# Seven-product stage of a Fourier and sliding-window kernel: second halves lag ten products, low parts earlier, half of the gate moved beside it

## The chip, the cores and the metric

The kernel runs on one core of a Trainium2 chip. The metric is the device time of one execution in microseconds. Before the change its median is 891.25 us over three runs (891.09 to 891.96). One execution was also profiled; its own time was 883.99 us, and the profile spans 882.3 us of it. Five engines run side by side: PE multiplies matrices, DVE (VectorE), ACT (ScalarE) and POOL (GpSimd) work on elements, SP only issues transfers. POOL and ACT issue transfers too. The profile shows PE's weight loads apart, as PEld.

## The reference

With x of 2048 rows by 512 columns, the output mixes two branches row by row:

```
g = sigmoid((x * gate_w).sum(-1))
a = x @ dft_hid_re.T ;  b = x @ dft_hid_im.T            # 2048 x 512 each
A = dft_seq_re @ a - dft_seq_im @ b                     # 2048 x 2048 by 2048 x 512, twice
q, k, v = x @ wqkv      (32 heads of 16, scale 1/4)
B = softmax(q k^T, keys j with 0 <= i - j < 256) v @ wo
out = g * A + (1 - g) * B
```

All inputs and the output are float32.

## The kernel before, in words

**Numbers in two parts.** An operand of a large product is split into a high part (type fp32r, one copy or cast on ACT, called `hi` or the first half of a `big` tile) and a low part (the original minus the high part, one subtraction on DVE or POOL). A product is the sum of three: high by high, high by low, low by high.

**The dense stream.** The generator `dense` yields after each step; `halves64` is its main part. It runs every product as two halves of 64 rows, so that one matmul of an upper half and one of a lower half stand side by side on PE. A step issues one matmul of a part's first half and one of a part's second half; the second halves come `DELAY` = 6 steps later. In order, the parts are 38 of 12 steps (q and k of all heads, v), then eight pairs of 42 steps, then the products with the sequence matrices, 24 steps each. 1896 first halves make 1902 steps.

**A pair** (function `pair`) computes a and b for two blocks of 128 rows by a two-by-two block product with seven products instead of eight, six steps each. They accumulate in four places in PSUM, `o1`, `o7`, `o5`, `o6`; the first three take two products each. When a half of a product ends and others will still accumulate in the same place, `product` either calls the place's `mid` (ACT copies the sum to `U` or `V`, or DVE adds it to `V`) or lets ACT copy one column of it to `tick` (L530). The other half's first matmul waits for that copy.

**Operands of a pair.** `x_load(p)` brings 512 KB of x to a `raw` tile through POOL's queue. `x_sums(p)` makes four sums of quarters on POOL (L748 to L751). `x_split` makes four high parts on ACT (L761) and their low parts (all recorded at L142): number 0 (512 columns) and number 3 (256 columns) on DVE, 1 and 2 (512 columns) on POOL. The parts go to six places in `XT`. At a pair's end the sums of `U`, `V` and PSUM are formed on DVE (L810, L813, L835, L845) and one on POOL (`fourth`, L816), and are stored to `ab_scr`.

**Due times.** `after(n, fn)` emits `fn` n steps after now. All five engines take their instructions in the order of emission, so what stands ahead on an engine's queue delays what stands behind. `prepare` emits everything for the pairs relative to t, the first pair's first step; `b` is the start of the pair before p.

**The attention** is interleaved with the dense stream: about every seven steps a pair of score matmuls (L356), whose row minimum DVE takes at once (L360, `junk` and `ml`), and a pair of transposed scores (L415), whose exponential ACT takes (L418) and POOL masks (L420, L424); every 56 steps or so a product with v (L438).

**The gate** g needs x once more in rows: `gate_load(j)` brings two blocks of 128 rows to a `raw` tile through POOL's queue, `gate(tb)` multiplies one by the gate's weights and sums the row on DVE (L257). All 16 blocks run while q and k are computed. `home` (3072 columns) holds the q and k parts on their way out; later `load_ab` uses it for a and b on their way in (`reload`).

Of the kernel before, what the change touches and what calls it, by code (L numbers as in the profile page):

```python
# [7 lines left out]
F32 = mybir.dt.float32  # L8
# [6 lines left out]
P = 128  # L15
S = 2048
D = 512
# [24 lines left out]
AHEAD = 216  # L42
SC = 10, 14, 9, 13, 8, 12, 0, 11, 15, 4, 1, 5, 2, 6, 3, 7
# [3 lines left out]
def fnet_window_mix(ctx: ExitStack, tc: tile.TileContext, xT, xp, x, wqk, wv, wr, wi, cr, ci, wo, gw, out):  # L47
# [197 lines left out]

    def gate_load(j):
        if j == 0:
            gwb.append(ev.tile([P, D], F32, name="ev"))
            with behind("sp"):
                ld(gwb[0], bass.AP(tensor=gw.tensor, offset=gw.offset, ap=[[0, P], [1, D]]))  # L250
        GX[j] = raw_tile()
        for c in range(2):
            ld_pool(GX[j][:, HALVES[c]], x[2 * j + c])

    def gate(tb):
        t = GX[tb // 2][:, HALVES[tb % 2]]
# [68 lines left out]
    stage = [f(home[:, 512 * k:512 * k + 512]) for k in range(6)]  # L325
# [208 lines left out]
    def halves64(groups):  # L534
# [3 lines left out]
        steps.append(len(first) + DELAY)  # L538
        ends = {}
        for d, order in ((0, first), (DELAY, second)):  # L540
            for t, (part, _) in enumerate(order):
                if part.out.load:
                    ends[part.out] = max(t + d, ends.get(part.out, 0))
# [3 lines left out]
        for t in range(len(first) + DELAY):  # L547
# [3 lines left out]
            if t < len(first):  # L551
# [6 lines left out]
            if t >= DELAY:  # L558
                part_b, i_b = second[t - DELAY]
                product(part_b, 1, i_b)  # L560
# [75 lines left out]
    def dense():  # L636
# [116 lines left out]
        XSPOTS = [(k, 2) for k in range(4)] + [(k, 3) for k in range(2)]  # L753

        def x_split(n, p, k):
            def go():
                t = tiles[p, k] = XT[XSPOTS[(4 * p + k) % 6]]
                m = 256 if k == 3 else 512
                raw = (RAWS["x", p][:, :512], RAWS["s", p][:, :512],
                       RAWS["s", p][:, 512:], RAWS["x", p][:, 768:])[k]  # L760
# [4 lines left out]
        def prepare():  # L765
# [32 lines left out]
        def pair(p):  # L798
# [21 lines left out]
            def place(t, k):  # L820
                ab[t] = XT[((2, 3), (3, 3))[k]] if p == 6 else XT[XSPOTS[(26 + k) % 6]]
# [11 lines left out]
            def p7_end(o):  # L833
# [4 lines left out]
                else:  # L838
                    d = place(t2, 1)
                    after(3, nc.scalar.copy, d[:, 0], e)  # L840
# [479 lines left out]
```

## Time and profile before

| what | value |
|---|---|
| median of three runs | 891.25 us |
| profiled execution, its span | 883.99 us, 882.3 us |
| busy of the span: PE, DVE, ACT, POOL | 833.7, 578.4, 437.5, 445.7 us |
| q, k, v in `halves64` | 33.5 to 184.7 us |
| the eight pairs | 184.7 to 344.2 us |
| products with the sequence matrices in `halves64` | 344.2 to 730 us |

The bounds of the stages were found by counting the matmuls of L525, two to a step: 912 in the first stage, 672 in the pairs. Times in the views are microseconds from the start of the span, unless they say ns. In a view of waits a row is the engine and line that waited, the releaser, and the sum, the count and the longest in us.

### The profile page before, as it was taken

How to read it: one execution, taken by the hardware profiler on the slowest of the kernel's cores; microseconds unless marked ns; L12 is line 12 of the kernel's file. 1: busy time of each engine (PE TensorE's matmuls, PEld its weight loads, DVE VectorE, ACT ScalarE, POOL GpSimd, SP SyncE). 2: the span in 40 equal slices, each digit the busy share in tenths (PEclk: the TensorE clock that was granted, in tenths of full speed). 3: DMA queues.
4: the chain of work that ended last, by engine and by line, in shares of the span. 5: the costliest groups of instructions: out<-in, count | busy, mean ns of one | idle time of the engine just before them, and what ended most of it. 6: DMA issues, size and time to landing. Idle time of an engine off the chain costs nothing.

```text
span 882.3 us, 19861 instructions
## 1 busy us (share of the span) xinstructions
PE 833.7 (94%) x7202; PEld 644.6 (73%) x7202; DVE 578.4 (66%) x1558; ACT 437.5 (50%) x878; POOL 445.7 (51%) x764
## 2 busy tenths in 40 slices
PE   9999989997988887999999999999999999899998
PEld 7898756765656556677777777767777777788886
DVE  6378777866865668765676665678787626455452
ACT  6236555565444456565565555556555564231310
POOL 5005546567764785354344444446554545675530
PEclk9999999999997998999999999999999999999999
DMA  9888997884454357456564665787887566875631
GB/s 340 256 241 242 324 316 233 280 299 134 149 158 117 114 177 249 144 146 187 152 182 128 189 182 171 220 238 218 237 245 224 162 191 198 241 246 162 205 111 48
DMA packets 112434, 177.72 MB, mean 201 GB/s; under 512 B 34640, under 2 KB 44368, under 8 KB 112336
## 3 DMA queue, kind: packets, MB, share of 16 engines
q1 hardware_dynamic: 97344, 129.14, 47.4%
q0 software_dynamic: 13024, 46.14, 17.2%
q10 hardware_dynamic: 1968, 1.18, 0.5%
q8 instruction: 56, 0.92, 0.5%
q14 instruction: 42, 0.34, 0.1%
HBM read 114.56 MB, written 61.60 MB: 200 GB/s over the span
## 4 chain that ended last, share of the span: by engine, by line
PE 67%; DVE 11%; DMA 8%; issue 6%; ACT 4%; POOL 2%; SPq 1%; ACTq 0%; DVEq 0%; POOLq 0%
PE d L525 35%; PE o L438 9%; PE dc L581 8%; PE t L1145 5%; PE s L356 5%; DVE junk L360 4%; PE t L415 3%; PE d L568 2%; DMA qk_scr<-home 2%; DVE big L142 2%; DMA raw<-ci 2%; DMA ring<-qk_scr 2%; ACT pt L418 2%; DVE lo L158 1%; DMA home<-ab_scr 1%
## 5 line engine op out<-in xcount | busy, mean ns | idle before, releaser
L360 DVE CUSTOM_DVE_ANT_0 junk<-s,mask 128x384 f32<-128x384 f32 (+2 forms) x512 | 271.7, 531 | 174.8 <-PE s L356 163.7
L525 PE MATMUL d<-big,hi 64*128 64x512 f32 x1920 | 337.2, 394 | 0.0
L420 POOL TENSOR_SCALAR_AFFINE_SELECT pt<-pt 128x256 f32<-128x256 f32 x256 | 117.9, 461 | 287.5 <-ACT pt L418 221.6
L418 ACT ACTIVATE pt<-t 128x768 f32<-128x768 f32 (+2 forms) x256 | 197.6, 772 | 130.3 <-PE t L415 122.2
L525 PEld LDWEIGHTS d<-big,hi 64*128 64x128 f32 x1920 | 189.0, 187 | 27.9 <-issue 0.7
L525 PE MATMUL d<-big,lo 64*128 64x512 f32 x960 | 199.9, 394 | 0.0
L356 PE MATMUL s<-ring,ring 48*128 48x384 f32 (+2 forms) x512 | 106.8, 364 | 12.5 <-DVE ml L360 8.6
L525 PE MATMUL d<-hi,big 64*128 64x512 f32 x352 | 97.5, 408 | 10.9 <-ACT tick L530 10.8
L525 PEld LDWEIGHTS d<-big,lo 64*128 64x128 f32 x960 | 96.4, 187 | 13.4
L415 PE MATMUL t<-ring,ring 50*128 50x384 f32 (+2 forms) x512 | 95.1, 332 | 3.9 <-ACT tick L530 3.8
L424 POOL TENSOR_SCALAR_AFFINE_SELECT pt<-pt 128x256 f32<-128x256 f32 x224 | 97.3, 434 | 0.0
L157 ACT CAST hi<-raw 128x512 fp32r<-128x512 f32 x134 | 82.2, 618 | 27.6 <-DMA raw<-ci 15.4
L581 PE MATMUL dc<-big,hi 128*128 128x512 f32 x284 | 91.7, 392 | 0.0
L438 PE MATMUL o<-pt,vt 128*32 128x384 f32 (+2 forms) x1408 | 85.7, 391 | 3.0 <-DVE ml L360 2.8
L158 DVE TENSOR_TENSOR lo<-raw,hi 128x512 fp32r<-128x512 f32 x102 | 80.7, 791 | 10.1 <-ACT hi L157 9.8
L356 PEld LDWEIGHTS s<-ring,ring 48*128 48x128 f32 x512 | 58.0, 187 | 39.6 <-DVE ml L360 19.6
L525 PE MATMUL d<-big 64*128 64x512 f32 x384 | 81.2, 414 | 4.5 <-ACT tick L530 3.0
L438 PEld LDWEIGHTS o<-pt,vt 128*32 128x32 f32 x1408 | 42.5, 111 | 49.9 <-issue 30.0
L525 PEld LDWEIGHTS d<-hi,big 64*128 64x128 f32 x352 | 55.1, 191 | 23.8 <-ACT tick L530 20.3
L415 PEld LDWEIGHTS t<-ring,ring 50*128 50x128 f32 x512 | 55.3, 186 | 16.6 <-ACT tick L530 5.1
L525 PEld LDWEIGHTS d<-big 64*128 64x128 f32 x384 | 52.2, 190 | 18.0 <-ACT tick L530 15.6
L158 POOL TENSOR_TENSOR lo<-raw,hi 128x512 fp32r<-128x512 f32 x32 | 43.0, 1354 | 42.5 <-ACT hi L157 42.3
(150 smaller groups left out, 1123.4 us busy)
## 6 DMA issues: line engine op xcount, KB each, us to landing
ring<-qk_scr SPq DMA_DIRECT2D x128, 192.0 KB
qk_scr<-home SPq DMA_DIRECT2D x32, 512.0 KB
raw<-cr POOLq DMA_DIRECT2D x32, 512.0 KB, 5.2
r_scr<-ev SPq DMA_DIRECT2D x44, 256.0 KB
raw<-ci POOLq DMA_DIRECT2D x18, 512.0 KB, 6.1
qk_scr<-home SPq DMA_DIRECT2D x32, 256.0 KB
ev<-l_scr SPq DMA_DIRECT2D x32, 256.0 KB
o_scr<-ev SPq DMA_DIRECT2D x32, 256.0 KB
```

What stands on the lines that cost most here:

```text
L157: jobs.append(lambda c=c: nc.scalar.copy(hi[:, c], raw[:, c]))
L158: jobs.append(lambda c=c: (nc.gpsimd if FIN else nc.vector).tensor_sub(lo[:, c], raw[:, c], f(hi[:, c])))
L356: nc.tensor.matmul(ps[:, h, :w], ring[0][r, p, j * P:j * P + P], ring[1][r, p, k0:k0 + w], start=True, stop=True)
L360: mark("dve", nc.vector.tensor_tensor_reduce(out=junk[:, :w], in0=ps[:, h, :w], in1=mask[:, WIN - w:], scale=1.0, scalar=3e38, op0=OP.add, ...
L415: nc.tensor.matmul(ps[:, h, :w], ring[1][r, p, q0:q0 + P], ring[0][r, p, q0:q0 + w], start=True, stop=True)
L418: nc.scalar.activation(pt[:, ph, :w], ps[:, :, :w], AF.Exp, scale=-1.0)
L420: nc.gpsimd.affine_select(a, a, pattern=[[0, 2], [1, P]], compare_op=OP.is_ge, fill=0.0, base=0, channel_multiplier=-1)
L424: nc.gpsimd.affine_select(a, a, pattern=[[0, 2], [-1, P]], compare_op=OP.is_gt, fill=0.0, base=0, channel_multiplier=1)
L438: nc.tensor.matmul(o[32 * j:32 * j + 32, (a - 4 * c) * P:(e - 4 * c) * P], v[:, kb % 4, 32 * j:32 * j + 32], PT[G * NB + kb][:, j, (a - kb ...
L525: nc.tensor.matmul(o.ps, lhs[r], rhs[r], start=start, stop=end and o.left == 0, skip_group_check=True)
L581: nc.tensor.matmul(ps, w[a][:, i % 8 * 128:i % 8 * 128 + 128], ab[SC[i]][:, b], start=i == ends[0] and a + b == 0, stop=i == ends[1] and a ...
L1145: nc.tensor.matmul(ps, o[:, a, c], fin(n, b, c), start=start and c == 0 and a + b == 0, stop=c == 1 and a == 1, skip_group_check=True)
```

## The change

**Second halves.** `HOLE` = 4 empty steps are put into the list of second halves where the pairs begin, and four into the list of first halves where the products of 24 steps begin. Between the two, a second half comes ten steps after its first half. There are 1906 steps in place of 1902.

**Low parts and sums.** For the pairs from the third on, relative to `b`: load at -6 (was -8), sums at 14 (22), high parts 0, 1, 2, 3 at 12, 26, 32, 16 (26, 31, 39, 35); each low part comes three steps later as before. The first two pairs have times of their own. Parts 0 to 2 alternate between two sets of three places; part 3 has half of `XT[2, 3]` to itself.

**Gate.** The blocks 0 to 7 stay beside q and k; 8 to 15 are loaded at t + 22, 49, ... into `home` and multiplied 22 steps after their load, with a second copy of the gate's weights in `home`. `U` and `V` move from `ev` tiles to `home`, and `mid` is called at once instead of two steps later. `reload` has five places instead of six, and its casts come two steps later.

At the start of the fourth pair, PE's queue held before the change (`d` are places in PSUM, `big` and `hi`/`lo` the operands):

```order
L525 MATMUL d_3279<-hi_2730,big_561 128x512
L525 MATMUL d_3249<-big_429,big_593 128x512
L525 MATMUL d_3428<-hi_1938,big_479 128x512 [waits DVE_49]
L525 MATMUL d_3279<-hi_2730,big_561 128x512 [waits Activation_49]
L356 MATMUL s_3433<-ring1_298,ring0_297 128x384 [waits DVE_49]
```

and now:

```order
L534 MATMUL d_3402<-hi_1913,big_522 128x512 [waits DVE_49]
L534 MATMUL d_3221<-big_429,big_619 128x512
L534 MATMUL d_3402<-lo_1914,big_522 128x512
L534 MATMUL d_3221<-big_429,big_619 128x512
L365 MATMUL s_3407<-ring1_298,ring0_297 128x384 [waits DVE_49]
L365 MATMUL s_3407<-ring1_298,ring0_297 128x384
L534 MATMUL d_3402<-hi_1913,big_522 128x512
L534 MATMUL d_3221<-big_444,big_619 128x512
L534 MATMUL d_3402<-hi_1913,big_522 128x512
L534 MATMUL d_3221<-big_429,big_619 128x512
L534 MATMUL d_3402<-lo_1914,big_522 128x512
L534 MATMUL d_3252<-hi_2697,big_505 128x512 [waits Activation_49]
```

The row that waits for the copy to `tick` is the fourth of the first piece: it reopens `d_3279` one step after the last matmul of the same place's first half, which is the piece's first row. In the second piece the last matmul of the first half of `d_3252` stands two rows ahead of the first row; the row that reopens `d_3252` and waits for ACT is the last one. Four full steps and a pair of scores have come between.

On DVE, around the end of the fourth pair before the change (`junk,ml` are the row minima, 128x256 is low part 3):

```order
L813 TENSOR_TENSOR ev<-d,ev 128x512
L360 ISA junk,ml<-s,mask 128x384
L360 ISA ml 128x1
L360 ISA junk,ml<-s,mask 128x384
L360 ISA ml 128x1
L142 TENSOR_TENSOR big<-raw,big 128x256
L835 TENSOR_TENSOR ev<-d,ev 128x512
```

and around the start of a pair now:

```order
L868 TENSOR_TENSOR ev<-d,home 128x512
L266 SCALAR_TENSOR_TENSOR home,gl<-home 128x512
L143 TENSOR_TENSOR big<-raw,big 128x512
L369 ISA junk,ml<-s,mask 128x384
L369 ISA ml 128x1
L369 ISA junk,ml<-s,mask 128x384
L369 ISA ml 128x1
L143 TENSOR_TENSOR big<-raw,big 128x256
```

Low part 3 has moved from the stretch between L813 and L835, a pair's end, to the stretch behind L868, the end of the pair before; a gate (L266) stands ahead of low part 0.

POOL's queue at a pair's end, before:

```order
L72 DMA raw<-xp 128x1024
L142 TENSOR_TENSOR big<-raw,big 128x512
L816 TENSOR_TENSOR ev<-ev 128x512
L420 AFFINE_SELECT pt<-pt 128x2x128
L424 AFFINE_SELECT pt<-pt 128x2x128
L142 TENSOR_TENSOR big<-raw,big 128x512
```

and now:

```order
L143 TENSOR_TENSOR big<-raw,big 128x512
L429 AFFINE_SELECT pt<-pt 128x2x128
L433 AFFINE_SELECT pt<-pt 128x2x128
L73 DMA home<-x 128x512
L143 TENSOR_TENSOR big<-raw,big 128x512
L73 DMA raw<-xp 128x1024
L839 TENSOR_TENSOR home<-home 128x512
```

Both low parts of POOL now stand ahead of the next load of x and of `fourth`; the issue of a gate's load stands between them.

```diff
+HOLE = 4
...
+    def gate_place(tb, t):
+        GX[tb] = t
+        ld_pool(t, x[tb])
...
-    stage = [f(home[:, 512 * k:512 * k + 512]) for k in range(6)]
+    stage = [f(home[:, 512 * k:512 * k + 512]) for k in (2, 3, 0, 5, 4)]
...
-        steps.append(len(first) + DELAY)
+        at = next(i for i, p in enumerate(second) if p[0].n < 12)
+        second[at:at] = [None] * HOLE
+        at = next(i for i, p in enumerate(first) if p[0].n > 12)
+        first[at:at] = [None] * HOLE
+        steps.append(len(second) + DELAY)
...
-        XSPOTS = [(k, 2) for k in range(4)] + [(k, 3) for k in range(2)]
+        def spot(k):
+            return XT[((0, 2), (1, 2), (2, 2), (3, 2), (0, 3), (1, 3))[k % 6]]
+
+        def home_spot(k):
+            return home[:, 512 * k:512 * k + 512]
 
         def x_split(n, p, k):
             def go():
-                t = tiles[p, k] = XT[XSPOTS[(4 * p + k) % 6]]
+                t = tiles[p, k] = spot(3 * p + k) if k < 3 else XT[2, 3][:, :, p % 2 * 256:p % 2 * 256 + 256]
...
                 b = t + 42 * p - 42
-                after(t - 38 if p == 0 else t + 14 if p == 1 else b - 8, x_load, p)
-                after(b + (20 if p == 0 else 29 if p == 1 else 22), x_sums, p)
-                for k, n in enumerate((30, 35, 40, 38) if p == 1 else (26, 31, 39, 35)):
+                load, add, *splits = {0: (4, 20, 24, 30, 36, 52), 1: (14, 27, 27, 36, 40, 30)}.get(
+                    p, (-6, 14, 12, 26, 32, 16))
+                after(b + load, x_load, p)
+                after(b + add, x_sums, p)
+                for k, n in enumerate(splits):
                     x_split(b + n, p, k)
+            after(t + 20, lambda: gate_weights(f(home_spot(1))))
+            for i in range(8):
+                after(t + 22 + 27 * i, gate_place, 8 + i, f(home_spot(2 + i % 2)))
+                after(t + 44 + 27 * i, gate, 8 + i)
...
             def keep(into):
                 def go(o):
-                    u = ev.tile([P, 512], F32, name="ev")
+                    u = f(home_spot(5 - (into is U) if p < 7 else 1)) if into is U or p < 7 else ev.tile(
+                        [P, 512], F32, name="ev")
                     nc.scalar.copy(u, o.ps)
                     into.append(u)
-                return shortly(go)
+                return go
...
-            o5 = Out(shortly(p5_end), 2, mid=shortly(p5_mid))
+            o5 = Out(shortly(p5_end), 2, mid=p5_mid)
...
         def reload():
             w = [XT[dk, ss] for ss in range(2) for dk in range(4)]
-            x = [XT[XSPOTS[(28 + k) % 6]] for k in range(4)]
-            casts = [-5] * 6
...
+            x = [*map(spot, (3, 4, 5)), XT[2, 3]]
+            casts = [-5] * 5
...
-                at = max(n - 29, casts[-6] + 5)
+                at = max(n - 29, casts[-5] + 5, {8: 5, 12: 17, 0: 17}.get(sc, 0))
...
-            9: [lambda: gate_load(0)],
-            10: [lambda: gate_load(1)],
             11: [lambda: load_w(2, wqk[2])],
-            12: [lambda: gates(0, 1)],
...
+            12: [lambda: gate_load(0)],
+            14: [lambda: split_w(2), lambda: gates(0, 1)],
+            15: [lambda: gate_load(1)],
+            16: [lambda: load_w(3, wqk[3])],
+            17: [lambda: gates(2, 3)],
+            18: [lambda: split_w(3), lambda: gate_load(2)],
+            20: [lambda: gate_load(3), lambda: gates(4, 5), lambda: prepare()],
+            22: [lambda: gates(6, 7)],
```

More of the change, by code (lines that the diff above doesn't have):

```diff
@@ L244, in fnet_window_mix, with gate_weights @@
     GX = {}
+    def gate_weights(t):
+        gwb[:] = [t]
+        with behind("sp"):
+            ld(t, bass.AP(tensor=gw.tensor, offset=gw.offset, ap=[[0, P], [1, D]]))
     def gate_load(j):
         if j == 0:
[L248 to L251, printed above, removed]
+            gate_weights(ev.tile([P, D], F32, name="ev"))
+        t = raw_tile()
         for c in range(2):
-            ld_pool(GX[j][:, HALVES[c]], x[2 * j + c])
+            GX[2 * j + c] = t[:, HALVES[c]]
+            ld_pool(GX[2 * j + c], x[2 * j + c])
+    def gate_place(tb, t):
+        GX[tb] = t
+        ld_pool(t, x[tb])
     def gate(tb):
-        t = GX[tb // 2][:, HALVES[tb % 2]]
+        t = GX.pop(tb)
         nc.vector.scalar_tensor_tensor(t, t, 1.0, gwb[0], op0=OP.mult, op1=OP.mult,
@@ L537, in halves64 @@
                   for i in range(p.n)]
-        steps.append(len(first) + DELAY)
+        at = next(i for i, p in enumerate(second) if p[0].n < 12)
[3 more added lines that the diff above has]
+        steps.append(len(second) + DELAY)
         ends = {}
         for d, order in ((0, first), (DELAY, second)):
-            for t, (part, _) in enumerate(order):
-                if part.out.load:
-                    ends[part.out] = max(t + d, ends.get(part.out, 0))
+            for t, e in enumerate(order):
+                if e and e[0].out.load:
+                    ends[e[0].out] = max(t + d, ends.get(e[0].out, 0))
         fetches = {}
@@ L546, in halves64 @@
             fetches.setdefault(t - FETCH, []).append(o)
-        for t in range(len(first) + DELAY):
+        for t in range(steps[0]):
             taken[0] += 1
@@ L550, in halves64 @@
                 o.r = o.load()
-            if t < len(first):
+            if t < len(first) and first[t]:
                 part, i = first[t]
@@ L557, in halves64 @@
                 product(part, 0, i)
-            if t >= DELAY:
+            if t >= DELAY and second[t - DELAY]:
                 part_b, i_b = second[t - DELAY]
@@ L839, in p7_end @@
                     d = place(t2, 1)
-                    after(3, nc.scalar.copy, d[:, 0], e)
-                    after(6, nc.vector.tensor_sub, d[:, 1], e, f(d[:, 0]))
+                    after(8, nc.scalar.copy, d[:, 0], e)
+                    after(11, nc.vector.tensor_sub, d[:, 1], e, f(d[:, 0]))
             def p5_end(o):
@@ L885, in reload @@
             w = [XT[dk, ss] for ss in range(2) for dk in range(4)]
-            x = [XT[XSPOTS[(28 + k) % 6]] for k in range(4)]
-            casts = [-5] * 6
-            for n, sc, dst in ((27, 9, w[0]), (29, 13, w[1]), (31, 8, x[1]), (34, 12, w[2]), (37, 0, w[3]), (46, 4, w[4]),
-                               (50, 1, w[5]), (54, 5, x[0]), (60, 2, w[6]), (64, 6, w[7]), (68, 3, x[3]), (72, 7, x[2])):
-                at = max(n - 29, casts[-6] + 5)
+            x = [*map(spot, (3, 4, 5)), XT[2, 3]]
+            casts = [-5] * 5
+            for n, sc, dst in ((29, 9, w[0]), (31, 13, w[1]), (33, 8, x[1]), (36, 12, w[2]), (39, 0, w[3]), (48, 4, w[4]),
+                               (52, 1, w[5]), (56, 5, x[0]), (62, 2, w[6]), (66, 6, w[7]), (70, 3, x[3]), (74, 7, x[2])):
+                at = max(n - 29, casts[-5] + 5, {8: 5, 12: 17, 0: 17}.get(sc, 0))
                 casts.append(n)
@@ L915, in dense @@
             order[i].pre = lambda fns=fns: [fn() for fn in fns]
-        for p, k, fn in ((6, 1, pieces.load), (7, 0, lambda: (reload(), pieces.load())), (7, 1, pieces.split),
+        for p, k, fn in ((6, 4, pieces.load), (7, 0, lambda: (reload(), pieces.load())), (7, 1, pieces.split),
                          (7, 3, pieces.load), (7, 4, pieces.split), (7, 6, pieces.load)):
```

16 lines of the change are left out of this document (2 added, 14 removed).

## The prediction

> **What bounds the kernel now.** I read first the page's busy times: PE 94%, no other engine over 66%. Then the windows by stage, PE's half-height products (L525) alone; the columns are the stretch, its length, PE's and PEld's busy time with their instructions, granted clock, DMA share and GB/s:
>
> ```profile
> span 882.3 us, 19861 instructions
> ...
> PE 833.7 (94%) x7202; PEld 644.6 (73%) x7202; DVE 578.4 (66%) x1558; ACT 437.5 (50%) x878; POOL 445.7 (51%) x764
> ...
> 184.70:344.20 159.50, 114.52 (x674) 79.02 (x672) 0.97 0.53 166
> 400.00:550.00 150.00, 123.38 (x890) 81.37 (x886) 1.00 0.58 167
> 550.00:700.00 150.00, 119.53 (x860) 80.01 (x862) 1.00 0.76 222
> ```
>
> The eight pairs have 336 steps, 672 matmuls. They take 159.5 us, 0.475 us a step. Two later stretches with the same attention between the steps do 445 and 430 steps in 150 us, 0.337 and 0.349 us a step; 336 steps at those rates are 113 and 117 us. So the pairs carry 42 to 46 us that a step does not need. Where these go, the waits of PE's weight loads say, in the pairs, and in the last row in the stretch from 33.5 to 101 us (the row before it is the group of the copies to `tick` in the pairs):
>
> ```profile
> PEld d L525 <- ACT tick L530: 35.8, 51, 1.7
> PEld s L356 <- DVE ml L360: 7.9, 6, 2.6
> ...
> PEld s L376 <- DVE ml L360: 4.1, 2, 3.2
> ...
> L530 ACT COPY tick<-d 128x1 f32<-128x1 f32 x56 | 8.9, 158 | 12.1 <-PE d L525 11.7
> ...
> PEld d L525 <- ACT tick L530: 0.3, 1, 0.3
> ```
>
> 51 of the 56 copies to `tick` hold PE up in the pairs, 35.8 us in all, 0.70 us each. The same copy costs 0.3 us in all from 33.5 to 101 us, where six or more steps lie between a place's last first-half matmul and its first second-half one. In the pairs none lies between: a product has six steps and the second half comes six later. One such wait in the timeline (start, length, engine):
>
> ```profile
> 240.85 0.39 PE L525 MATMUL d<-hi,big 64*128 64x512 f32 x1
> 240.94 0.39 ACT L418 ACTIVATE pt<-t 128x256 f32<-128x256 f32 x1
> 241.22 0.40 ACT L403 COPY vt<-vr 128x256 f32<-128x256 f32 x1
> ...
> 241.51 0.17 ACT L530 COPY tick<-d 128x1 f32<-128x1 f32 x1
> ...
> 241.73 0.18 PEld L525 LDWEIGHTS d<-hi,big 64*128 64x128 f32 x1 [0.92 <-ACT tick L530]
> ```
>
> The last matmul ends at 241.24; ACT takes two other instructions first, copies for 0.17, and PE resumes at 241.73.
>
> The second loss is DVE's. PE waits 12.0 us for it in the rows above, and three of its instructions are far longer than their like, all low part 3 of a pair:
>
> ```profile
> L142 DVE TENSOR_TENSOR big<-raw,big 128x256 fp32r<-128x256 f32 x8 | 18.5, 2307 | 0.9 <-ACT big L761 0.9
> L142 DVE TENSOR_TENSOR big<-raw,big 128x512 fp32r<-128x512 f32 x7 | 5.5, 793 | 1.9 <-ACT big L761 1.9
> L813 DVE TENSOR_TENSOR ev<-d,ev 128x512 f32<-128x512 f32 x8 | 5.5, 685 | 0.0
> ...
> 221.56 5.22 DVE L142 TENSOR_TENSOR big<-raw,big 128x256 fp32r<-128x256 f32 x1
> ...
> 259.87 4.49 DVE L142 TENSOR_TENSOR big<-raw,big 128x256 fp32r<-128x256 f32 x1
> ...
> 283.76 5.36 DVE L142 TENSOR_TENSOR big<-raw,big 128x256 fp32r<-128x256 f32 x1
> ...
> 259.24 1.31 POOL L142 TENSOR_TENSOR big<-raw,big 128x512 fp32r<-128x512 f32 x1
> 260.50 1.28 POOL L816 TENSOR_TENSOR ev<-ev 128x512 f32<-128x512 f32 x1
> ...
> 264.04 0.58 POOL L424 TENSOR_SCALAR_AFFINE_SELECT pt<-pt 128x256 f32<-128x256 f32 x1
> ```
>
> 256 columns take 2.3 us on the mean, 512 only 0.79. The three long ones, 15.1 of 18.5 us, stand at a pair's end, where POOL runs without a break (259.24 to 264.62). DVE instructions that read PSUM and one tile (L813) take 0.685 us throughout. So it is the DVE instructions with both inputs in SBUF that are held while POOL runs.
>
> **The change part by part.** The sum is made against the profiled 883.99 us; the median is 7.3 us above it, and I add that at the end.
>
> *Ten steps of lag.* Between a place's last first-half matmul and the waiting one now lie four steps, 4 x 0.34 = 1.4 us. The wait is 0.70 us on the mean and 1.7 at the longest, so most is hidden under the other places' matmuls. Of 35.8 us some 0.05 us each is the ordinary gap between loads (2.5 us) and I leave 2 us for the long ones: **-31 us**. Bounds: -33, and 0 if ACT were late by all four steps each time. The cover is other work only as long as PSUM places come free: a place that was free 13 steps before its next use is now free nine before, 9 x 0.34 = 3.1 us, against a DVE addition of 0.685 us; that costs nothing unless DVE is held for 4.5 us.
>
> *The holes* add four steps: 4 x 0.34 = **+1.3 us**.
>
> *Low part 3 away from POOL's burst, the gate towards it.* Part 3 goes from b + 38 to b + 19, beside the sums on POOL; the low parts 0, which meet the sums now, take 0.79 us, so a meeting costs about 0.1. The eight gates come in its place: at 2, 29, 14, 41, 26, 11, 38 and 23 of the 42 steps, so that five lie in POOL's busy stretch (26 to 44: two low parts, a load's issue, `fourth`). Three of eight were held there before, so I expect about two holds. Of the 12.0 us I give half: **-6 us**; bounds -12 and +12 (four holds more at 3 us of PE). The clock's 0.97 over 159.5 us, 4.8 us of PE at most, follows such waits: **-1 us**.
>
> [...]
>
> *More work in the pairs.* Gates and loads that leave the first stage come here:
>
> ```profile
> L257 DVE SCALAR_TENSOR_TENSOR raw<-raw,ev x16: 681/686/689, 72.1 to 118.5; 128x512 f32<-128x512 f32 x16
> L72 POOL DMA_DIRECT2D raw<-x x16: 536/544/556, 38.4 to 107.3; - x16
> ...
> 184.70:344.20 159.50, 135.08 (x1152) 93.21 (x1150) 108.36 (x269) 82.08 (x191) 107.03 (x171) 0.97 0.53 166
> 550.00:700.00 150.00, 146.06 (x1432) 110.74 (x1426) 114.94 (x332) 84.81 (x156) 76.01 (x155) 1.00 0.76 222
> ```
>
> (In the last two rows PE, PEld, DVE, ACT, POOL.) DVE gets 8 x 0.77 = 6.2 us with the row sums, POOL 8 x 0.54 = 4.4. In a stage of 130 us, POOL's 107 + 4 are 85%, DVE's 108 - 13 + 6 are 78%. At 550 to 700 us DVE is at 77%, PE still goes at 0.349 us a step; but POOL is at 51% there, and no stretch shows it at 85%. Bounds 0 and +10.6 (all of it on the path): **+6 us**.
>
> *x nearer to its use.* The load goes from 34 steps ahead of ACT's first cast to 18, and on POOL's queue behind a low part:
>
> ```profile
> raw<-xp POOLq DMA_DIRECT2D x7, 512.0 KB, 5.3
> home<-ab_scr POOLq DMA_DIRECT2D x9, 256.0 KB, 8.3
> ...
> L72 POOL DMA_DIRECT2D raw<-xp x7 | 4.1, 592 | 0.0
> ```
>
> 18 steps of 0.38 us (the 128 us that I expect for 336) are 6.9 us; the low part ahead (1.28), the issue (0.59) and the landing (5.3) are 7.2. ACT then waits 0.3 to 1.3 us in seven pairs, and behind it stand exponentials and ticks. 2 to 9 us, none if PE's four steps cover it: **+5 us**. In `reload` two loads of a and b have 19 and 22 steps in place of 29, 6.5 to 7.5 us against 8.3 to land, and the second pair's x has 13 in place of 15: **+3 us** (0 to 5).
>
> *First stage.* Two megabytes of gate loads leave it. In it PE waits once for long:
>
> ```profile
> 72.00:126.00 54.00, 53.35 (x508) 40.66 (x506) 44.20 (x151) 31.73 (x62) 29.95 (x63) 1.00 0.95 296
> ...
> PE t L415 <- ACT tick L530: 3.8, 1, 3.8
> ...
> ACT home L105 <- DMA qk_scr<-home: 6.4, 3, 4.8
> ```
>
> ACT waits 4.8 us for a store of q and k behind transfers at a DMA share of 0.95, and PE 3.8 for ACT. Less to move helps, though the loads that stay shift later: **-2 us** (0 to -4.8). The gates themselves cost nothing there now: their DVE time lies under a PE that is busy 53.35 of 54 us.
>
> Sum: -31 + 1.3 - 6 - 1 + 6 + 5 + 3 - 2 = -24.7, so 859.3 profiled and **866.5 us** in the median. The pairs should then take about 132 us.
>
> **The rivals.** *The pairs reach the later stages' rate*: 117 us, with POOL and x no bound; -42.3 + 1.3 - 2 = -43, 848 us. For it: DVE at 77% did not slow PE at 550 us. Against it: POOL's 111 us in 117.
> *POOL and x's loads take the place of the ticks*: +10.6, +9 and +5 in place of +6, +5 and +3, and no hold saved: -14 to -7, about 879 us. For it speaks the load's 7.2 us in 6.9; against it, that ACT is busy only 82 of 159 us and can catch up.
> *The ticks wait as before*, because it is ACT that is late, not PE: 890 us. Against it: 1.4 us of cover for 0.70.
> *Slower: DVE is held all along.* 24 instructions with both inputs in SBUF (16 low parts, 8 gates) stand beside a POOL that is busy 85%. One hold costs PE up to 2.6 or 3.2 us. With the faster steps a hold of 4.5 us also outlasts the nine steps (3.1 us) that a PSUM place has. From nine holds more than the two counted the gain is gone; with twelve the time is 866.5 + 12 x 3 = 902 us. Against it: only 3 of 15 were held, and none beside the sums. [...]
>
> **How the numbers follow.** Forecast 0.48, the later stages' rate 0.16, POOL and x's loads 0.24, ticks as before 0.04, slower 0.08. The range of 853 to 886 us leaves out the faster half of the first rival, the ticks and the slow one, 0.20. A measurement of this kernel can tell about 0.2%, 1.8 us, from no change. Faster by more: the first three, 0.88; within it the ticks as before, 0.04; slower 0.08.
>
> **What would show it.** Right: L530 as releaser of PEld falls from 35.8 to under 5 us in the pairs; no 128x256 low part over 2 us; the pairs take 125 to 138 us; POOL's busy share there is over 80%. A wait of ACT's L777 (the casts, L761 before) for `raw<-xp` of more than 9 us would show x late. Gates (L266) of 4 us or more, with PE waiting for `ml`, would show the holds. Wrong would be ticks that still wait, a stage of over 145 us, or a gain that lies mostly outside the pairs.

## The result and the profile after

The changed kernel takes 882.85 us in the median (880.36 to 883.12, four runs), the kernel before 891.36 (891.09 to 891.96, four runs): a ratio of 0.9897, 95% interval 0.9879 to 0.9916. It gains 8.5 us. The forecast was a gain of 24.7 us, a time of 866.5.

The page of the changed kernel, its span and busy times:

```profile
span 880.6 us, 19850 instructions
...
PE 826.7 (94%) x7202; PEld 649.7 (74%) x7202; DVE 577.1 (66%) x1558; ACT 437.1 (50%) x878; POOL 444.0 (50%) x764
```

The windows by stage of the changed kernel, all instructions (columns: stretch, its length, busy time and instructions of PE, PEld, DVE, ACT, POOL, granted clock, DMA share, GB/s). The rows are the eight pairs, the first 72 steps behind them, the last stage from the end of `halves64` on:

```profile
182.80:331.20 148.40, 124.84 (x1146) 93.77 (x1143) 109.24 (x283) 79.33 (x186) 108.82 (x177) 0.94 0.60 184
331.20:364.80 33.60, 27.19 (x236) 20.59 (x236) 29.06 (x73) 19.09 (x39) 16.32 (x30) 0.90 0.67 201
722.70:880.60 157.90, 147.93 (x824) 122.76 (x822) 78.85 (x134) 40.46 (x87) 74.95 (x71) 0.98 0.54 171
```

The pairs fell from 159.5 to 148.4 us, not to 132. Their granted clock is lower than before, 0.94 against 0.97. The waits of PE's weight loads in the pairs say what took the ticks' place (engine, line and releaser; sum, count and longest in us), and below them three rows of ScalarE's and VectorE's waits in the same stretch:

```profile
PEld s L365 <- DVE ml L369: 11.8, 8, 3.7
PEld t L424 <- ACT pt L427: 7.1, 2, 3.6
...
PEld s L385 <- DVE ml L369: 3.9, 2, 3.0
PEld s L365 <- ACT pt L427: 2.3, 4, 1.8
PEld d L534 <- ACT tick L539: 1.4, 2, 1.0
```

```profile
ACT big L777 <- DMA raw<-xp: 10.9, 4, 3.5
...
DVE big L143 <- ACT big L777: 8.0, 5, 3.3
DVE home L266 <- DMA home<-x: 3.1, 2, 2.1
```

The ticks did what was forecast: 35.8 us in 51 waits became 1.4 us in two. In their place stand few waits that are long: a score product waits 3.7 us for DVE's row minimum, a transposed score 3.6 us for ACT's exponential. Two events show how they arise. The first is the timeline of the changed kernel around 305 us:

```profile
297.34 0.58 POOL L73 DMA_DIRECT2D raw<-xp  x1
...
305.55 0.62 ACT L777 CAST big<-raw 128x512 fp32r<-128x512 f32 x1 [3.48 <-DMA raw<-xp]
306.07 0.80 ACT L427 ACTIVATE pt<-t 128x768 f32<-128x768 f32 x1
...
306.93 0.45 PE L424 MATMUL t<-ring,ring 50*128 50x384 f32 x2 [3.13 <-ACT pt L427]
```

The load of x is issued at 297.34, and ACT's cast waits for it until 305.55, 8.2 us later. The exponential stands behind the cast on ACT's queue, and PE stands still for 3.13 us. What that does to the clock is in the windows of 3.4 us before and after:

```profile
304.00:307.40 3.40, 0.47 (x4) 0.47 (x6) 1.17 (x4) 1.85 (x4) 0.46 (x2) 1.00 0.56 210
307.40:310.80 3.40, 3.40 (x20) 2.77 (x20) 2.70 (x8) 2.29 (x6) 3.24 (x5) 0.50 0.13 50
```

PE works 0.47 us of the first 3.4, and for the next 3.4 its clock is 0.50. So this wait costs 3.1 us and then, as an estimate from the half clock, some 1.7 us more. Not every long stop does. PE stops six times for 1.8 to 3.4 us in these pairs; with four of the stops the clock falls (1.80, 2.54, 3.13 and 3.43 us), with two it does not (3.10 and 3.18). The falls begin at 208.4, 266.45, 283.5 and 307.4 us: 17, 22 and 29 times 3.413 us behind the first, as if the clock were set anew at the lines of a fixed grid. In the four windows of this grid that end with a fall PE works 0.47 to 1.61 us. The stops of 3.10 and 3.18 us are each cut by a line, and PE works 1.54 to 2.11 us in the windows on its two sides. Here are those around the first of them, another late load of x, which stops PE for 3.10 us until 234.02:

```profile
228.88:232.29 3.41, 2.03 (x20) 1.46 (x16) 1.84 (x5) 0.16 (x1) 0.00 (x0) 1.00 1.01 347
232.29:235.70 3.41, 1.68 (x16) 1.48 (x18) 2.38 (x6) 3.06 (x7) 1.67 (x4) 1.00 0.37 135
```

So what a stop costs in clock seems to be in part a matter of where it falls.

The second event is a gate block that is held (DVE and POOL in the timeline of the changed kernel):

```profile
202.81 5.65 DVE L266 SCALAR_TENSOR_TENSOR home<-home 128x512 f32<-128x512 f32 x1
...
203.10 1.31 POOL L839 TENSOR_TENSOR home<-home 128x512 f32<-128x512 f32 x1
204.35 1.28 POOL L143 TENSOR_TENSOR big<-raw,big 128x512 fp32r<-128x512 f32 x1
...
206.31 1.25 POOL L143 TENSOR_TENSOR big<-raw,big 128x512 fp32r<-128x512 f32 x1
207.52 0.40 POOL L429 TENSOR_SCALAR_AFFINE_SELECT pt<-pt 128x256 f32<-128x256 f32 x1
207.88 0.85 POOL L433 TENSOR_SCALAR_AFFINE_SELECT pt<-pt 128x256 f32<-128x256 f32 x1
...
209.61 0.69 PE L365 MATMUL s<-ring,ring 48*128 48x384 f32 x2 [3.43 <-DVE ml L369]
```

A block that takes 0.63 to 0.69 us beside q and k takes 5.65, beside seven POOL instructions that follow on each other. It ends at 208.46, 0.27 us before the last of them. The row minimum of the scores is queued behind it on DVE, and PE waits 3.43 us for that. The groups by shape of the changed kernel's pairs give the sums:

```profile
L266 DVE SCALAR_TENSOR_TENSOR home<-home 128x512 f32<-128x512 f32 x8 | 15.5, 1941 | 3.1 <-DMA home<-x 3.1
...
L143 DVE TENSOR_TENSOR big<-raw,big 128x256 fp32r<-128x256 f32 x8 | 5.7, 707 | 0.2 <-ACT big L777 0.2
```

Low part 3 is free of holds (18.5 us before, 5.7 now), and the gate has taken its place.

### The profile page after: what moved, and what is told of

Same layout as the page of the kernel before. It is cut to its first block, busy times and chain, and to the rows that moved or that the text cites. A ratio compares the mean times of both kernels' runs of the same rounds, so it can differ in the third digit from the quotient of the medians.

```text
span 880.6 us, 19850 instructions
## 1 busy us (share of the span) xinstructions
PE 826.7 (94%) x7202; PEld 649.7 (74%) x7202; DVE 577.1 (66%) x1558; ACT 437.1 (50%) x878; POOL 444.0 (50%) x764
## 4 chain that ended last, share of the span: by engine, by line
PE 68%; DMA 10%; DVE 10%; issue 5%; POOL 5%; ACT 3%; ACTq 0%; SPq 0%; DVEq 0%; POOLq 0%
PE d L534 35%; PE o L447 8%; PE dc L594 8%; PE s L365 5%; PE t L1162 5%; PE t L424 3%; DVE junk L369 3%; PE d L581 2%; DMA qk_scr<-home 2%; DMA raw<-ci 2%; DMA raw<-xp 2%; DVE big L143 2%; ACT pt L427 2%; DVE lo L159 1%; POOL big L143 1%
## 5 line engine op out<-in xcount | busy, mean ns | idle before, releaser
L429 POOL TENSOR_SCALAR_AFFINE_SELECT pt<-pt 128x256 f32<-128x256 f32 x256 | 114.2, 447 | 303.3 <-ACT pt L427 246.7
L365 PE MATMUL s<-ring,ring 48*128 48x384 f32 (+2 forms) x512 | 100.2, 366 | 24.1 <-DVE ml L369 18.1
L534 PE MATMUL d<-hi,big 64*128 64x512 f32 x352 | 100.6, 412 | 2.4 <-ACT tick L539 1.4
L424 PE MATMUL t<-ring,ring 50*128 50x384 f32 (+2 forms) x512 | 88.8, 333 | 9.0 <-ACT pt L427 6.2
L433 POOL TENSOR_SCALAR_AFFINE_SELECT pt<-pt 128x256 f32<-128x256 f32 x224 | 95.8, 428 | 0.0
L365 PEld LDWEIGHTS s<-ring,ring 48*128 48x128 f32 x512 | 53.2, 187 | 52.5 <-DVE ml L369 30.3
L159 DVE TENSOR_TENSOR lo<-raw,hi 128x512 fp32r<-128x512 f32 x102 | 78.8, 773 | 10.2 <-ACT hi L158 10.0
L424 PEld LDWEIGHTS t<-ring,ring 50*128 50x128 f32 x512 | 51.2, 188 | 23.2 <-ACT pt L427 7.7
L534 PEld LDWEIGHTS d<-hi,big 64*128 64x128 f32 x352 | 58.8, 195 | 7.9 <-ACT tick L539 2.3
L534 PE MATMUL d<-lo,big 64*128 64x512 f32 x176 | 62.4, 408 | 0.0
```

The source lines that it names most:

```text
L159: jobs.append(lambda c=c: (nc.gpsimd if FIN else nc.vector).tensor_sub(lo[:, c], raw[:, c], f(hi[:, c])))
L365: nc.tensor.matmul(ps[:, h, :w], ring[0][r, p, j * P:j * P + P], ring[1][r, p, k0:k0 + w], start=True, stop=True)
L424: nc.tensor.matmul(ps[:, h, :w], ring[1][r, p, q0:q0 + P], ring[0][r, p, q0:q0 + w], start=True, stop=True)
L429: nc.gpsimd.affine_select(a, a, pattern=[[0, 2], [1, P]], compare_op=OP.is_ge, fill=0.0, base=0, channel_multiplier=-1)
L433: nc.gpsimd.affine_select(a, a, pattern=[[0, 2], [-1, P]], compare_op=OP.is_gt, fill=0.0, base=0, channel_multiplier=1)
L534: nc.tensor.matmul(o.ps, lhs[r], rhs[r], start=start, stop=end and o.left == 0, skip_group_check=True)
```

## The experiments

Theory A: the ticks had hidden other lateness; what PE no longer waits for at a tick, it waits for at a held DVE or at x that comes late. Theory B: the lag is worth its 31 us, and the other parts of the change lose 20. Thirteen runs were made, the first of them of the kernel before once more. The table has the stages of each one's profiled execution, in us: the start of the pairs, their length, the rest of `halves64`, the last stage, and the span; then the median of its runs and the ratio to the kernel before, run on the same chip, with its 95% interval. "Gate in" means eight blocks beside the pairs, "first" all sixteen ahead of them.

| version | lag | gate | x load | start | pairs | rest | last | span | median | ratio |
|---|---|---|---|---|---|---|---|---|---|---|
| before, first profile | no | first | before's | 184.7 | 159.5 | 385.9 | 152.2 | 882.3 | 891.36 | |
| before, second profile | no | first | before's | 185.0 | 165.5 | 386.5 | 151.7 | 888.7 | | |
| e2, lag alone | 10 | first | before's | 184.6 | 157.9 | 390.1 | 158.4 | 891.0 | 889.61 | 0.998 (0.9956 to 1.0004) |
| the change | 10 | in | b - 6 | 182.8 | 148.4 | 391.5 | 157.9 | 880.6 | 882.85 | 0.9897 (0.9879 to 0.9916) |
| e3 | no | in | b - 6 | 182.8 | 152.7 | 386.4 | 153.0 | 874.9 | 879.41 | 0.987 (0.9829 to 0.9912) |
| e4 | 10 | first | b - 6 | 184.2 | 139.6 | 389.9 | 156.1 | 869.8 | 873.98 | 0.9798 (0.9767 to 0.983) |
| e5 | 10 | in | b - 16 | 183.2 | 135.2 | 391.3 | 155.6 | 865.3 | 868.6 | 0.9778 (0.9728 to 0.9828) |
| e6, gate moved | 10 | in | b - 6 | 183.3 | 144.7 | 390.7 | 155.0 | 873.7 | 876.16 | 0.9851 (0.9806 to 0.9896) |
| e7 | 10 | first | b - 16 | 186.3 | 126.1 | 396.0 | 154.5 | 862.9 | 863.76 | 0.9697 (0.9673 to 0.9721) |
| e8 | no | first | b - 6 | 185.2 | 151.6 | 388.0 | 151.4 | 876.2 | 879.11 | 0.9886 (0.9846 to 0.9925) |
| e9 | no | first | b - 16 | 184.5 | 152.0 | 387.0 | 151.6 | 875.1 | 880.4 | 0.9883 (0.9849 to 0.9917) |
| e10, steps without lag | no | in | b - 6 | 182.4 | 154.1 | 391.0 | 156.0 | 883.5 | 888.58 | 0.9966 (0.9937 to 0.9996) |
| e11 | no | in | b - 16 | 183.1 | 153.1 | 387.8 | 153.1 | 877.1 | 880.48 | 0.9891 (0.9864 to 0.9918) |
| e12, two empty steps | 8 | first | b - 16 | 188.5 | 128.2 | 391.0 | 154.1 | 861.8 | 861.15 | 0.9663 (0.9625 to 0.9702) |
| e14, lag of 8 kept | 8 | first | b - 16 | 186.5 | 128.3 | 397.3 | 151.4 | 863.5 | 863.22 | 0.9693 (0.9655 to 0.9731) |

### The kernel before once more

> The kernel before, unchanged, for a second profile: the first one (883.99 us) lies 7.3 us under the median of the kernel, so it cannot say where the median lost 8.5 us. If the pairs and the copies to `tick` are the same in every execution, the pairs take 157 to 162 us again with 33 to 38 us of tick waits, and the missing 5 to 7 us lie outside them, after 730 us most likely (152.2 us in the first profile, 157.9 with the change). The rival: the pairs themselves vary by several us, 164 us or more here.

Its span was 888.7 us, of which the pairs took 165.5. The first profile of before, on which the prediction rests, was some 7 us faster than its median, and 6 of these lie in the pairs. The second profile's row of the pairs, and the two waits that carry the argument:

```profile
185.00:350.50 165.50, 139.22 (x1152) 97.16 (x1150) 107.77 (x270) 82.08 (x190) 106.51 (x171) 0.94 0.52 163
```

```profile
PEld d L525 <- ACT tick L530: 35.1, 50, 2.3
PEld s L356 <- DVE ml L360: 10.1, 5, 2.8
```

This is the rival outcome of its expectation: the pairs themselves vary. The waits for the ticks are the same, those for DVE 2.2 us longer. What differs most is the clock, 0.94 against 0.97: it stands at one half for 21.2 us of these pairs, for 11.0 us in the first profile. By an estimate from that, 10.2 us at half rate, the clock makes 5.1 of the 6.0 us. So a difference of a few us in the pairs between single profiles says little; the differences below are larger, or are backed by medians.

### The lag alone, and the change without the lag

```diff
 # e2: the lag only, in the kernel before (the loop behind these lines skips the empty steps)
+HOLE = 4
...
+        at = next(i for i, p in enumerate(second) if p[0].n < 12)
+        second[at:at] = [None] * HOLE
+        at = next(i for i, p in enumerate(first) if p[0].n > 12)
+        first[at:at] = [None] * HOLE
...
 # e3: the changed kernel
-HOLE = 4
+HOLE = 0
```

> The kernel before with the ten steps of lag alone; x, low parts and gate as before. Theory A (the ticks hid other lateness: what PE no longer waits for ACT it waits for DVE and for exponentials): the tick waits fall from 35.8 under 5 us, but the pairs fall only to 140 to 150 us and the time to 876 to 886 us. Theory B (the lag is worth its 31 us and the other edits of the change lose 20 of it again): the pairs fall to 125 to 132 us, the time to 860 to 868 us.

> The changed kernel without the lag (no empty steps, second halves six steps behind throughout); all else as changed. Theory A: the tick waits are back at 30 to 38 us and the pairs take 155 to 162 us; the time is 888 to 895 us, no better than before, since the other edits bring little by themselves. Theory B: the other edits lose, so the time is above 895 us.

Both theories missed. The lag alone gives nothing that can be told (889.61 us, ratio 0.998), and the change without the lag is as fast as with it (879.41 us; the two intervals overlap). In e2 the ticks' wait fell, and the wait for DVE stayed, with longer single waits:

```profile
PEld d L526 <- ACT tick L531: 12.5, 9, 4.4
PEld s L357 <- DVE ml L361: 12.3, 6, 3.8
```

```profile
L143 DVE TENSOR_TENSOR big<-raw,big 128x256 fp32r<-128x256 f32 x8 | 19.3, 2414 | 0.0
```

Low part 3 is held as before the change (19.3 us for eight). The clock in these pairs is 0.92. The pairs gain 7.6 us against the second profile of before, and the two stages behind them lose 10.3.

In e3 the ticks wait 38.3 us, and PE waits far less for what it waited for in the changed kernel (11.8 and 3.9 us for the row minima there, 7.1 for the exponentials):

```profile
PEld d L534 <- ACT tick L539: 38.3, 53, 3.5
...
PEld s L365 <- DVE ml L369: 2.4, 4, 0.9
PEld s L385 <- DVE ml L369: 1.5, 2, 0.9
```

53 waits of 0.7 us on the mean leave the clock at 0.98, and its one stretch at half rate (192.1 to 198.9) begins at the longest of them, 3.5 us:

```profile
182.80:335.50 152.70, 133.45 (x1154) 91.88 (x1151) 102.98 (x287) 82.34 (x190) 110.80 (x176) 0.98 0.60 183
198.90:335.50 136.60, 121.05 (x1075) 83.12 (x1075) 94.88 (x261) 74.18 (x172) 101.88 (x161) 1.00 0.58 173
```

Not all of this is cover: without the lag there is also less lateness to cover. The eight gates take 8.8 us in e3 and 15.5 in the change, and ACT waits 5.7 us for x where it waited 10.9:

```profile
L266 DVE SCALAR_TENSOR_TENSOR home<-home 128x512 f32<-128x512 f32 x8 | 8.8, 1101 | 0.0
```

### The gate, the load of x, and both

```diff
 # e4: the changed kernel with all sixteen gate blocks beside q and k, as before
-            after(t + 20, lambda: gate_weights(f(home_spot(1))))
-            for i in range(8):
-                after(t + 22 + 27 * i, gate_place, 8 + i, f(home_spot(2 + i % 2)))
-                after(t + 44 + 27 * i, gate, 8 + i)
... (blocks 8 to 15 are loaded and multiplied beside q and k again)
 # e5: the changed kernel with x ten steps earlier for the third pair and on; e7 is e4 and e5
-                    p, (-6, 14, 12, 26, 32, 16))
+                    p, (-16, 14, 12, 26, 32, 16))
 # e6: the changed kernel with the gate blocks, and their loads, on other steps
-            for i in range(8):
-                after(t + 22 + 27 * i, gate_place, 8 + i, f(home_spot(2 + i % 2)))
-                after(t + 44 + 27 * i, gate, 8 + i)
+            for i, n in enumerate((51, 67, 93, 109, 135, 151, 177, 193)):
+                after(t + n - 22, gate_place, 8 + i, f(home_spot(2 + i % 2)))
+                after(t + n, gate, 8 + i)
```

> The changed kernel with all 16 gate blocks beside q and k again, as before the change; lag, x and low parts as changed. The gates in the pairs took 15.5 us of DVE in place of 5.5 (two of eight were held for 4.5 and 5.7 us). Theory A with the gate as the main new holder: the pairs fall from 148 to 138 to 143 us and the time to 874 to 879 us; the first stage pays 0 to 3 us. Rival (whatever DVE has with two inputs, or a cast, next to POOL's run is held, the gate or another): the pairs stay within 145 to 150 us, the time within 880 to 886 us.

> The changed kernel with the parts of x of products 2 to 7 loaded 10 steps earlier (16 steps before the product's steps begin instead of 6). Theory C (the ticks' many short waits were replaced by few long ones, and x that comes late is one of them): ScalarE's wait for raw<-xp in the pairs falls from 10.9 us to under 3, PE's wait for t<-pt (7.1 us) to under 3, one or two half-clock stretches less, the pairs 141 to 145 us instead of 148.4, and the time 875 to 879 us. Rival D (what PE waits for there is only handed on: the next late value, the held low parts or the ticks, takes its place): x is in time, but s and the ticks wait longer by as much, and the time is 881 to 885 us.

> The changed kernel with the eight gate blocks of the pairs put on steps at which GpSimd has no sums beside them. Theory C (a VectorE instruction is held only while GpSimd runs several instructions back to back, and the gate fell into such a burst): the eight gate instructions fall from 15.5 us to 5 to 8 us, no one over 2 us, PE's wait for s (11.8 us) falls by 3 to 6 us, and the time is 877 to 880 us. Rival D (other low parts and casts are held in its place, since GpSimd has the same work to do): some other VectorE instruction of the pairs is held for 3.5 us or more, the sum of holds is as before, and the time is 881 to 885 us.

> The lag, all sixteen gate blocks ahead of the pairs, and x loaded 10 steps earlier. In the version with x early and half of the gate in the pairs VectorE waited 6.1 us for the gate's x, and TensorE 9.1 us for s. Theory C (each long wait is a cost of its own as long as none covers another): without the gate in the pairs the wait for s falls under 4 us, the pairs are 128 to 132 us, the first stage gives 1.5 to 2.5 us back, and the time is 863 to 867 us. Rival D (the next late value takes its place): the pairs are 134 to 137 us and the time 869 to 872 us.

e4 came to 873.98 us, at the lower end of theory A: without the gate beside them the pairs take 8.8 us less. e5 gained more than theory C said: 868.6 us and 13.2 us off the pairs. ACT's wait for x fell to 5.9 us, not under 3; that is one wait, for the second pair's x, whose load did not move. e7 has both and does what theory C expected, 863.76 us; its pairs are even shorter than forecast, 126.1 us at a clock of 0.99. The pairs of e4 and of e7, which differ only in x's load:

```profile
184.20:323.80 139.60, 124.35 (x1147) 97.02 (x1144) 93.88 (x264) 79.62 (x185) 102.88 (x168) 0.93 0.58 181
186.30:312.40 126.10, 117.49 (x1147) 91.54 (x1144) 90.49 (x262) 77.89 (x184) 102.43 (x166) 0.99 0.65 198
```

Of the 13.5 us between them PE is idle for 6.6 less and busy for 6.9 less, the latter with a clock of 0.99 in place of 0.93: about half of the price of late x, as an estimate from these rows, is paid in clock. The longest waits left in e7:

```profile
PEld s L365 <- ACT tick L539: 2.6, 1, 2.6
...
PEld t L424 <- ACT pt L427: 2.3, 1, 2.3
```

No wait of PE's loads for a value is longer than 2.6 us there. e5 showed one more cost of the gate in the pairs: with x early no block is held over 1.5 us, but DVE waits for the gate's own rows of x, which come through POOL's queue (VectorE's waits in e5's pairs):

```profile
DVE home L266 <- DMA home<-x: 6.1, 3, 3.0
```

e6 bears out theory C on the hold, and in part rival D on what follows. Groups and waits of e6's pairs:

```profile
L266 DVE SCALAR_TENSOR_TENSOR home<-home 128x512 f32<-128x512 f32 x8 | 7.1, 884 | 0.0
L377 DVE CAST mlh<-ml 128x64 fp32r<-128x64 f32 x6 | 5.8, 965 | 0.1
```

```profile
PEld t L424 <- ACT pt L427: 11.3, 3, 4.4
```

The gate falls from 15.5 to 7.1 us, no block over 1.9. One cast is held for 3.7 us, but it was held as long in the change, so no new hold took the gate's place. ACT's wait for x rises from 10.9 to 19.1 us. In e4, with no gate there at all and shorter pairs, it rises too, to 14.1; in e6 the gate's loads have also moved on the queue that brings x, and how much either does was not tried. The time, 876.16 us, is below what either had.

### The same without the lag

e8, e9 and e11 are e4, e7 and e5 with `HOLE = 0`.

> Neither the lag nor the gate in the pairs: the rest of the change alone. If the lag and the gate act independently, the gate's 8.9 us come off the version without the lag: 870 to 872 us, pairs 143 to 145 us, and 4 to 5 us less than with the lag in the first 72 steps of the stage behind and in the last stage each. If the lag is worth its ticks once the long waits are gone (theory B in a weaker form), the ticks wait 30 us or more again, the pairs are 150 to 155 us, and the time is 877 to 882 us, slower than the same version with the lag (873.98 us).

> As the version with the lag, all gate blocks first and x early, but without the lag. Theory C: the ticks wait 36 us or more and cover the rest, the pairs are 148 to 152 us and the time is 875 to 879 us, as with half of the gate in the pairs (without the lag neither the gate nor x is worth over 3 us). Rival E (x and gate are worth as much without the lag): pairs under 140 us, time 862 to 868 us.

> The changed kernel with x loaded 10 steps earlier and without the lag of ten. Theory C (the lag's ticks are worth 12 to 16 us in the pairs once x is in time, and the lag costs 4 to 7 us behind them): the ticks wait 36 us or more, the pairs are 147 to 151 us (135.2 with the lag), and the time is 874 to 878 us, 6 to 9 above the same version with the lag (868.6). Rival E (x in time is worth the same with and without the lag, 13 to 14 us): the pairs are 139 to 141 us and the time 865 to 867 us, so that the lag is worth nothing there either.

These three settle the pairs. Their lengths, without and with the lag:

| | no lag | lag of ten | the lag's worth |
|---|---|---|---|
| gate in, x late | 152.7 | 148.4 | 4.3 |
| gate first, x late | 151.6 | 139.6 | 12.0 |
| gate in, x early | 153.1 | 135.2 | 17.9 |
| gate first, x early | 152.0 | 126.1 | 25.9 |

The medians follow in the same order: with the lag the time is 3.4 us longer in the first row and 5.1, 11.9 and 16.6 shorter in the others, 6 to 9 us behind the pairs' gain throughout.

Without the lag the pairs take 152 to 153 us whatever is done with gate and x: the ticks wait (36.7 us in e9), and what is late beside them costs PE little. With the lag each late value counts at once, 9 us for the gate and 13 us for x. e8 spoke against the first line of its expectation, that lag and gate act independently, and for the second; e11 and e9 spoke for theory C, with times 1 to 3 us above its ranges.

The rest of the change, low parts above all, needs the lag in the same way. e2 and e7 have the lag and all gate blocks first, and their pairs take 157.9 and 126.1 us, 31.8 less with the rest of the change and x early. Without the lag the same step, from the kernel before to e9, is worth 7.5 or 13.5 us by the two profiles of before.

e9's row of the ticks, beside e7's 1.7 us in two:

```profile
PEld d L534 <- ACT tick L539: 36.7, 53, 3.3
```

### What the lag costs behind the pairs

```diff
 # e10: the changed kernel; both lists get the empty steps where the products of 24 steps begin
-        at = next(i for i, p in enumerate(second) if p[0].n < 12)
+        at = next(i for i, p in enumerate(second) if p[0].n > 12)
 # e12: e7 with
-HOLE = 4
+HOLE = 2
 # e14: e12, and no empty steps among the first halves
-        at = next(i for i, p in enumerate(first) if p[0].n > 12)
-        first[at:at] = [None] * HOLE
```

> The changed kernel with the four empty steps put into both halves' lists at one and the same place, ahead of the long parts of the stage behind: 1906 steps as in the change, but the second halves lag six products' steps as before. If what the lag costs outside the pairs comes from the four steps (and the time-tabled loads and casts that move against the matmuls by them), the first 72 steps behind the pairs take 33 to 34 us and the last stage 157 to 158 us as in the change, the ticks wait 35 us or more in the pairs, and the time is 883 to 888 us. If it comes from the lag itself (values that come later by four steps, a second half that is still working when its tile is wanted), these are 31 and 153 us as without the lag, and the time is 878 to 881 us.

> The lag, all gate blocks first and x early, with two empty steps instead of four (second halves eight steps behind instead of ten). If two steps already cover the tick's latency, as its waits without the lag are 0.7 us each against 0.6 us that two steps take, the ticks wait 5 us or less, the pairs are within 3 us of the version with four, the stage behind and the last stage give 2 to 5 us back, and the time is 1 to 3 us under that version's. If eight is too short, the ticks wait 12 us or more and the time is 2 to 6 us above it.

> As the version with two empty steps, all gate blocks first and x early, but the second halves stay eight steps behind to the end: the first halves have no empty steps where the products end, so that no stretch there has one half of the matmuls alone; the steps are as many. If what the lag costs behind the pairs is this stretch (TensorE half empty and its clock halved after it), the first 72 steps behind the pairs take 31 to 32 us instead of 34.5, the half-clock stretches at 318 to 336 us go, and the time is 857 to 860 us. If it comes from values that are wanted at the same time-tabled step but come two to four steps later (the first product of the next stage, the exponentials of the last), these steps take 34 us or more, the last stage stays at 154 us, and the time is 861 to 864 us.

e10 has the four steps and no lag. Its pairs are as without the lag (154.1 us), and behind them it loses as much as with it: 391.0 and 156.0 us against 386.4 and 153.0 in e3, 7.6 us together, and 888.58 us in the median, 9.2 above e3's. So four steps in the list cost 7 to 8 us behind the pairs, far more than the 1.3 us of their matmuls. The first 72 steps behind the pairs, in e3 and in e10:

```profile
335.50:366.60 31.10, 25.43 (x238) 18.34 (x240) 27.04 (x68) 17.05 (x35) 16.21 (x29) 1.00 0.63 192
```

```profile
336.50:370.40 33.90, 27.40 (x239) 20.44 (x237) 29.29 (x72) 17.59 (x37) 16.22 (x30) 0.90 0.64 186
```

The longer one has a granted clock of 0.90, by which some 6.8 us of it are at half rate, and the last stage waits longer for its exponentials. PE's wait there in e3, the change and e10:

```profile
PE t L1162 <- ACT ex L143: 2.3, 1, 2.3
```

```profile
PE t L1162 <- ACT ex L143: 5.2, 1, 5.2
```

```profile
PE t L1162 <- ACT ex L143: 4.2, 1, 4.2
```

e12's ticks wait between its two outcomes:

```profile
PEld d L534 <- ACT tick L539: 8.0, 18, 2.2
```

The pairs take 128.2 us, 2.1 more than with four steps, and the median is 861.15 us (856.5 to 863.78) against 863.76. These two cannot be told apart. e14 keeps the lag to the end, so that no half of the matmuls stands alone behind the pairs. Its last stage is back at 151.4 us, but the rest of `halves64` grows to 397.3, and the first 72 steps take 35.7: the second of its two outcomes. The empty stretch is therefore not what costs it. Which of the values on time-tabled steps is late there was not found.

## Why the prediction was wrong

The direction was right and the time lies inside the range of 853 to 886 us, but the gain was a third of the one forecast. Most of the mechanisms were named; what failed is their prices, and that they were taken as independent. By its terms, against the second profile of before, whose span is nearest to its median:

**Ten steps of lag, -31.** Right in mechanism: L539 as releaser of PEld is at 1.4 us, under the 5 that were named. In size it is -25.9 us where gate and x are out of the way (e9 to e7) and -4.3 in the change itself (e3 to the change). The step that failed is that this term was added to the others as if they did not touch it. The holds of DVE were priced by half of the 12.0 us that PE waits for them now, under the ticks' cover, and not by what they cost once the ticks are gone. The cover was the 0.7 us that PE lost at each of some 51 ticks.

**x nearer to its use, +5: mis-sized; it is +13** (13.2 from e5 to the change, 13.5 from e7 to e4). This term was reckoned with the faster steps, and it still came out too small. The working gave ACT a wait of 0.3 to 1.3 us in seven pairs. It is 10.9 us in four, the longest 3.5. The load issued at 297.34 took 8.2 us until the cast where 5.9 were reckoned (0.59 issue, 5.3 to land), and ACT had come to the cast 4.7 us after the issue, where the working left 5.6 (6.9 less 1.28 for the low part ahead). Behind the cast stood the exponential, as the text said. PE stopped 3.10 and 3.13 us for it, and behind one of the two stops the clock was halved, a price that the term did not hold. The sign that it named for this, a wait of L777 over 9 us, came.

**Low part 3 and the gate, -6, and more work in the pairs, +6: together 0; measured -7.5 to -13.5 and +9.** Low part 3 is rid of its holds (no one over 1 us). What of the change is neither lag, gate nor late x leaves pairs of 152.0 us in e9, from 159.5 or 165.5. But the gate beside the pairs costs 8.8 us (e4) or 9.1 (e7 against e5). "About two holds" was right to the number: 5.65 and 4.47 us, and a cast of 3.71 us that was not thought of. Nor was the gate's own wait for x (3.1 us in the change, 6.1 in e5).

**The clock, -1: wrong in sign.** It fell from 0.97 to 0.94 against the profile that the prediction used; against the second one it did not change.

**The holes, +1.3, and the reload, +3: mis-sized; together +11.2** (5.0 in the rest of `halves64`, 6.2 in the last stage, against the second profile). e10 puts 7.6 us of it on the four steps alone. Which value is late there stays open.

**First stage, -2:** the pairs start 2.2 us earlier. Right: the six kernels with the gate in start them at 182.4 to 183.3 us, all others at 184.2 to 188.5.

The rows add up: -2.2 - 17.1 + 5.0 + 6.2 = -8.1 us, from a span of 888.7 to 880.6. The 17.1 us of the pairs can be taken in single steps: -13.5 from before to e9, -25.9 for the lag, +9.1 for the gate, +13.2 for x. Laid beside the forecast of -24.7, the 16.6 us that are missing are 8.2 of x, 6.9 behind the pairs and 5.1 of the lag; low parts, gate and clock did 3.4 better. This holds for this order of steps, which has the lag in before gate and x, and for single profiles, of which those of before differ by 6 us.

Of the rivals, the one that put POOL and x's loads in the ticks' place (879 us, 0.24) came nearest, 4 us low, and had the late x right. POOL itself was no bound: it is busy 108.82 of 148.4 us, 73%, not over 80. In e7 it is busy 102.43 of 126.1, 81%, and the pairs still run at 0.375 us a step. Of "DVE held all along" the two holds came, not the twelve. The rate of the later stages, 117 us, was not reached by any version; e7's 126.1 is the nearest. Of the signs of being wrong that the prediction named, one came: a stage of over 145 us.

The reading in the prediction, that it is DVE's instructions with both inputs in SBUF that are held, was too narrow: in the change a cast, which has one input, was held for 3.71 us.

## What to carry to other kernels

When the most frequent wait is taken away, ask of every other queue how late it would be if the waiting engine came by as much sooner: without the lag, the placing of the gate and of x's load changed the pairs by 1.5 us at most, with it by 9 and 13 each. Many short waits are a poor price list for few long ones, since a long stop can also cost clock after it, as four of six did in the change, with a clock of 0.50 behind them. Where steps carry a time table, an empty step moves everything behind it: four of them cost 7 to 8 us in e10, not their own 1.3.

The version to take from these runs has the lag of eight or ten, all gate blocks first and x ten steps earlier: 861.15 or 863.76 us, 3.0 to 3.4% under the kernel before.

## What the hardware showed

A hold of a DVE instruction outlasts single POOL instructions (5.65 us over seven of them), but it does not always last until POOL pauses. That gate ended 0.27 us before POOL's run did. In the change a cast of 64 columns, 0.19 us in the median, was held for 3.71 us until 263.56, and POOL ran on to 264.22. What ends a hold was not found.

PE's clock was 1.00 from 198.9 us to the end of e3's pairs, with 49 waits for ticks of 0.67 us on the mean and 1.4 at the longest. It was 0.94 in the change's pairs, where loads wait for ticks, row minima and exponentials less often, but up to 3.7 us at a time. From the start of the pairs to 30 us behind their end, the falls of the clock begin at whole multiples of 3.413 us from each other, to 0.1 us: in the change at 208.43, 266.45, 283.52, 307.41 and 334.72 us (17, 22, 29 and 37 behind the first), in the first profile of before at 264.94, 343.45 and 350.28 (23 and 25), in e4 8, 17, 23, 29 and 37, in e2 3, 10, 14, 20, 26, 33 and 43 behind the first. Whether that is why the two profiles of before, whose loads wait 35.8 and 35.1 us for the ticks, differ in clock, 0.97 and 0.94, was not shown. These are readings of traces of versions that differ in more than the one thing; none was tried by itself.
